# Dhidden products two hidden chunks ahead, `kvbd` transposed on TensorE instead of by DMA, and loads respread around the last MLP chunk, in a fused transformer-block backward kernel

## Chip, cores, metric

One core of one Trainium2 chip. The metric is the device time of one execution in microseconds. Timed comparisons run both kernels alternately on the same chip. Several chips were used, so times are compared only within one set of rounds. Each run also has a mean granted clock of TensorE, 1.000 being full; a loss of 1.7 us out of 860 shows there as 0.998.

## The reference

One pre-norm block on 2048 tokens of width 640: linear attention with 32 heads, then a SwiGLU MLP with 1728 hidden units. The kernel returns the block's output and, for a given `grad_out`, the gradients of `x` and of all five weights, in bf16.

```python
def _fwd_reference(A_x, A_wqkv, A_wo, B_x, B_w1, B_w3, B_w2):
    # A: qkv = x @ wqkv; phi(t) = where(t > 0, t + 1, exp(t)) + 1e-6
    #    kv = sum_s phi(k) v ; o = phi(q) kv / (phi(q) z) ; return o @ wo
    # B: h = silu(x @ w1) * (x @ w3) ; return h @ w2
    h = x + _A_ref(_layernorm(x), A_wqkv, A_wo)
    return h + _B_ref(_layernorm(h), B_w1, B_w3, B_w2)

_out, _vjp = jax.vjp(_f, A_x, A_wqkv, A_wo, B_w1, B_w3, B_w2)
return (_out, *_vjp(grad_out))
```

## The kernel before

The instruction order of every engine is written out by hand. These stages matter here:

1. q, k, v and the key-value sums (0 to 76 us). The sums are kept as `kvbd`, where a mask leaves each head only its own block.
2. The first attention outputs: token tiles 0 to 3, mixed with the last q tiles (76 to 101 us). Each tile goes through a chain over several engines: `nd` on TensorE, `o_t` on VectorE, transpose on TensorE, `oT` on ScalarE, `at` on TensorE, statistics and `hn` on VectorE, transpose `trh` on TensorE.
3. The MLP in four token chunks `c` of 512, each in 14 hidden chunks `fc` of 128 (f chunks), with the gradient through the activation (101 to 360 us). "dhidden product" below means `w2T` times the transposed `grad_out`, five matmuls of 512 columns (`mlp_ghh`).
4. The gradient of `w2`, called `gw` (360 to 420 us). It reads `hb`, the hidden activations loaded transposed. The inputs of stage 5 are loaded meanwhile: `w13a` and `w13b` (the transposed `w1` and `w3`, with a small remainder called the tail), `kvbdT` (the transposed `kvbd`), and `ggb` (the gradients that stage 3 stored in DRAM as `gg_d`).
5. The gradients through the MLP's first product (`ghn`) and through the attention, token tile by token tile (424 to 600 us).
6. The remaining weight gradients and the gradient of `x`.

All plain DMA loads and most DMA transposes (`dmaT`) are issued in order from SyncE's queue.

```python
# stage 1: once, at the start
V.memset(kvbd[:], 0.0)
make_mask()                                  # GpSimd: one memset, ten selects
...
# stage 2: the hand-written order of the first attention outputs
for f, t in ((q_late, 8), (q_late, 9), (f2_ndo, 0), (q_late, 10), (f2_ot, 0), (f2_ndo, 1), (q_late, 11),
             (f2_at0, 0), (f2_ot, 1), (f2_ndo, 2), (q_late, 12), (f2_hn, 0), (f2_at0, 1), (f2_ht, 0),
             ...
             (q_late, 14), (f2_hn, 2), (f2_at0, 3), (f2_ht, 2), (q_late, 15), (f2_hn, 3)):
    f(t)
mlp_ghh(0, 0)
f2_ht(3)
mlp_ghh(0, 1)
...
# stage 3
def mlp_ghh(c, fc):
    acc = mm5(w2T, fc, g2T[c])               # PSUM tag "mm", three buffers
    if fc % 2 == 0:
        ghh[fc // 2] = ew("ghh")
    A.copy(out=ghh[fc // 2][:, fc % 2, :], in_=acc[:])

def mlp(c, fc, between, done):
    if fc not in done:
        mlp_ghh(c, fc)
    gp = mm5(w1, fc, hnT[c])
    ...                                      # sig, s2, gate on ScalarE
    upp = mm5(w3, fc, hnT[c])
    A.copy(out=up[:, i, :], in_=upp[:])      # up: two buffers, stored to DRAM by SyncE
...
if fc == (9 if c == 0 else 3) and c + 1 < SC:
    load_g2T(c + 1)                          # DMA transpose of the next chunk's grad_out
if c == SC - 1 and fc == 0:
    for i in range(SC):                      # grad_out, 640 KB each
        dma(out=g2[:, i * TPC:(i + 1) * TPC, :], in_=goS[:, i * TPC:(i + 1) * TPC, :])
if c == SC - 1 and fc == 4:
    dmaT(out=woT[:], in_=A_wo[:, :])
...
# stage 4, in the loop over fc of the gradient of w2
if fc == 2:
    for m in range(DT):
        kvbd_T(m)                            # five DMA transposes
if fc == 3:
    load_hh(3)                               # DMA transpose
if fc == 5:
    load_w13()                               # two small tail loads, two large DMA transposes
if fc == 8:
    load_gg(0, 0, NG)                        # ggb, what ghn waits for
```

Of the kernel before, what the change touches and what calls it, by code (L numbers as in the profile page):

```python
# [9 lines left out]
P = 128  # L10
BF16 = mybir.dt.bfloat16
F32 = mybir.dt.float32
ALU = mybir.AluOpType
# [6 lines left out]
DH = D // H  # L20
DA = DH + 1
# [42 lines left out]
def kernel(  # L64
# [105 lines left out]

    mask = cp.tile([P, DT, M_MAX], BF16, name="mask")

    def make_mask():
        G.memset(mask[:], 1.0)
        for m, (a, b) in enumerate(M_H):
            v = mask[:, m, 0:M_W[m]].rearrange("p (h e) -> p h e", e=DA)

            G.affine_select(out=v, in_=v, pattern=[[-DH, b - a], [0, DA]], compare_op=ALU.is_ge, fill=0.0,
                            base=m * P - a * DH, channel_multiplier=1)
            G.affine_select(out=v, in_=v, pattern=[[DH, b - a], [0, DA]], compare_op=ALU.is_gt, fill=0.0,  # L180
                            base=a * DH + DH - m * P, channel_multiplier=-1)


    w1 = U2.tile([P, DT, FP], BF16, name="w1", tag="A")
# [4 lines left out]
    g2T = {}  # L189

    def load_g2T(c):
        g2T[c] = U2.tile([P, DT, W], BF16, name="g2T", bufs=2)
        dmaT(out=g2T[c][:], in_=goD[c * W:(c + 1) * W, :])

    def load_pqT(c):
# [88 lines left out]
    p1_norm(0)  # L284
    p1_tr(0)
    ln1.run(x_sb, 1, 2)
    V.memset(kvbd[:], 0.0)
    p1_norm(1)
    ln1.run(x_sb, 2, 4)
    make_mask()  # L290
    trickle += [lambda: dmaT(out=w2T[:, :, 0:F], in_=B_w2[:, :]), lambda: load_g2T(0)]
    for c0, c1 in ((0, 2), (2, 4), (4, 5)):
        trickle += load_w13(c0, c1)
# [3 lines left out]
    for t in range(ST):  # L297
        g, i = divmod(t, TPC)
        if i == 0:
            pkc[g] = p1.tile([P, TPC, D], BF16, name="pkc", bufs=2)  # L300
        k = p1_mm(t, D)
        if t + 2 < ST:
            p1_norm(t + 2)
        phi(k, pkc[g][:, i, :])
        if t + 1 < ST:
            p1_tr(t + 1)
        if i == 0 and g > 0:
            kv_group(g - 1, False)
        v = p1_mm(t, 2 * D)
        A.copy(out=va[g % 2][:, i, 0:C].rearrange("p (j h e) -> p j h e", j=2, e=DA)[:, :, :, 0:DH],  # L310
               in_=v[:, :, 0:HD].rearrange("p j (h e) -> p j h e", e=DH))
        if 4 <= t < 12:
            q_tile(t - 4)
        if t % 2 == 0 and t + 4 < ST:
            ln1.run(x_sb, t + 4, t + 6)
        if i == TPC - 1:
            sl = slice(g * TPC, (g + 1) * TPC)
            dma(out=pk_v[:, sl, :], in_=pkc[g][:])
            dma(out=va_v[:, sl, :], in_=va[g % 2][:])
        elif t >= 2 and trickle:  # L320
            trickle.pop(0)()
# [90 lines left out]
    def mm5(w, fc, rhs):  # L412
        acc = ps.tile([P, W], F32, name="mm", bufs=3)
        for c in range(DT):
            T.matmul(acc[:], lhsT=w[:, c, fc * P:(fc + 1) * P], rhs=rhs[:, c, :], start=(c == 0),  # L415
                     stop=(c == DT - 1))
        return acc

    def ew(name):
        return pa.tile([P, 2, W], BF16, name=name, bufs=2)  # L420
# [1 line left out]
    NAMES = ("sig", "s2", "gate", "up")  # L422
    ghh, pair = {}, {}

    def mlp_ghh(c, fc):
        acc = mm5(w2T, fc, g2T[c])
        if fc % 2 == 0:
            ghh[fc // 2] = ew("ghh")
        A.copy(out=ghh[fc // 2][:, fc % 2, :], in_=acc[:])  # L429

    def mlp(c, fc, between, done):

        k, i = divmod(fc, 2)
        if fc not in done:
            mlp_ghh(c, fc)
        gp = mm5(w1, fc, hnT[c])
        if i == 0:
            pair[k] = [ew(name) for name in NAMES]
        sig, s2, gate, up = pair[k]
        A.activation(sig[:, i, :], gp[:], AF.Sigmoid)  # L440
        A.activation(s2[:, i, :], gp[:], AF.Sigmoid, scale=-1.0)
        A.copy(out=gate[:, i, :], in_=gp[:])
        drain(1)
        between()
        drain(1)
        if fc < FT - 1:
            upp = mm5(w3, fc, hnT[c])
            A.copy(out=up[:, i, :], in_=upp[:])
        else:
            V.memset(up[FL:, i, :], 0.0)  # L450
            A.copy(out=up[:FL, i, :], in_=gp[FL:])
        if i == 1:
            mlp_pair(c, k, *pair.pop(k), ghh.pop(k))

    def store(dst, r0, c, k, src):
        cs = slice(c * W, (c + 1) * W)
# [58 lines left out]
        f2_nd(t)  # L515
        f2_o(t)

    for f, t in ((q_late, 8), (q_late, 9), (f2_ndo, 0), (q_late, 10), (f2_ot, 0), (f2_ndo, 1), (q_late, 11),
                 (f2_at0, 0), (f2_ot, 1), (f2_ndo, 2), (q_late, 12), (f2_hn, 0), (f2_at0, 1), (f2_ht, 0),
                 (f2_ot, 2), (f2_ndo, 3), (q_late, 13), (f2_hn, 1), (f2_at0, 2), (f2_ht, 1), (f2_ot, 3),  # L520
                 (q_late, 14), (f2_hn, 2), (f2_at0, 3), (f2_ht, 2), (q_late, 15), (f2_hn, 3)):
        f(t)
    p1.release()
    pa = pool("pa", "right")
    mlp_ghh(0, 0)
    f2_ht(3)
    mlp_ghh(0, 1)

    w2 = U1.tile([P, FT, D], BF16, name="w2", tag="D")
    V.memset(w2[64:, FT - 1, :], 0.0)  # L530

    def sides(tr):
        side = ({}, {})
        for i in range(TPC):
            k0 = 3 * i - (tr and i == TPC - 1)
            for k, pos, f in ((k0, 0, f2_ndo), (k0 + 1 - tr, 1, f2_ot), (k0 + 2, 1, f2_at), (k0 + 3, 0, f2_hn),
                              (k0 + 4 - tr, tr, f2_ht)):
                side[pos].setdefault(k, []).append((f, i))
        return side

    sides = sides(1)
    for c in range(SC):
        hhT[c] = pa.tile([P, FT, W], BF16, name="hhT", bufs=2)
        o2 = o2_steps(c - 1) if c > 0 else None

        def run_side(pos, fc):
            if c + 1 < SC:
                for f, i in sorted(sides[pos].get(fc, ()), key=lambda x: x[1]):
                    f((c + 1) * TPC + i)

        for fc in range(FT):
            mlp(c, fc, lambda: run_side(0, fc), (0, 1) if c == 0 else ())
            drain(1)
            if o2 and not (c == SC - 1 and fc == 5):
                next(o2, None)
            run_side(1, fc)
            drain(1)
            if c == 0 and fc in (1, 4, 7):
                a, b = {1: (0, 4), 4: (4, 8), 7: (8, 13)}[fc]
                dma(out=w2[:, a:b, :], in_=B_w2[a * P:b * P, :].rearrange("(c p) n -> p c n", p=P))  # L560
                if fc == 7:
                    dma(out=w2[0:FL, FT - 1, :], in_=B_w2[(FT - 1) * P:F, :])
            if fc == (9 if c == 0 else 3) and c + 1 < SC:
                load_g2T(c + 1)
            if c == SC - 1 and fc == 0:
                g2 = U1.tile([P, ST, D], BF16, name="g2", tag="Q")
                for i in range(SC):
                    dma(out=g2[:, i * TPC:(i + 1) * TPC, :], in_=goS[:, i * TPC:(i + 1) * TPC, :])
            if c == SC - 1 and fc == 4:
                woT = U1.tile([P, DT, D], BF16, name="woT", tag="W6")  # L570
                dmaT(out=woT[:], in_=A_wo[:, :])
    drain(1)
# [21 lines left out]
    load_hh(1)  # L594
    load_hh(2)
    wT = [U1.tile([P, FT, D], BF16, name="w13a", tag="D"), U1.tile([P, FT - 1, D], BF16, name="w13b", tag="S0")]
    tail = br.tile([P, DT, P], BF16, name="w13tail")

    def load_w13():
        dma(out=tail[:, :, 0:FL], in_=B_w1[:, F - FL:F].rearrange("(c p) f -> p c f", p=P))  # L600
        dma(out=tail[:, :, FL:P], in_=B_w3[:, 0:P - FL].rearrange("(c p) f -> p c f", p=P))
        dmaT(out=wT[0][:, 0:FT - 1, :], in_=B_w1[:, 0:F - FL])  # L602
        dmaT(out=wT[1][:], in_=B_w3[:, P - FL:F])  # L603

# [5 lines left out]

    kvbdT = br.tile([P, CT, D], BF16, name="kvbdT")

    def kvbd_T(m):
        dmaT(out=kvbdT[:, :, m * P:(m + 1) * P], in_=kvbd[:, m, :])

    ggb = {}

# [26 lines left out]
    for fc in range(FT - 1):  # L644
        b, i = divmod(fc, 4)
        if fc == FT - 2:
            sb = gw2_tail()
        acc = ps.tile([P, 2, 512], F32, name="gw", bufs=4)
        for j in range(2):
            for t in range(ST):  # L650
                T.matmul(acc[:, j, 0:HD], lhsT=hb[b][:, t, i * P:(i + 1) * P], rhs=g2[:, t, j * HD:(j + 1) * HD],  # L651
                         start=(t == 0), stop=(t == ST - 1))
            if fc == FT - 2 and j == 0:
                gw2_tail_out(sb)
        ob = br.tile([P, D], BF16, name="gw2o", bufs=2)
        A.copy(out=ob[:].rearrange("p (j n) -> p j n", j=2), in_=acc[:, :, 0:HD])
        A.dma_start(out=out_6[fc * P:(fc + 1) * P, :], in_=ob[:])
        if fc == 3:
            load_hh(3)
        if fc == 5:  # L660
            load_w13()
        if fc == 8:
            load_gg(0, 0, NG)
        if fc == 11:
            load_gg(1, 0, NG)
        if fc == 2:
            for m in range(DT):
                kvbd_T(m)
        if fc == FT - 3:
            w13_tail()  # L670
    ps.release()
# [457 lines left out]
```

## Time and profile before

| | kernel before |
|---|---|
| median of 3 runs | 864.53 us (863.66 to 865.08) |
| profiled span | 862.8 us |
| TensorE busy | 842.6 us |
| VectorE, ScalarE busy | 416.1, 322.8 us |
| longest waits of TensorE after the start | 3.2 (`ggb`), 2.3 (`up`) us |

How to read it: TensorE's busy time comes within 20.2 us of the span. The lines are shown in the prediction. A timeline line has start and length in us, then engine, line of the kernel, operation and tiles; `SPq` is the issuing on SyncE's queue, and brackets hold the idle time before and what ended it. A line that starts with a window ends with the granted clock, the DMA share and GB/s.

### The profile page before, as it was taken

Reading aid. Unit: us, or ns where it says so; the run is one execution under the profiler, and the core shown is the slowest. Engines: PE = TensorE matmul, PEld = TensorE weight load, DVE = VectorE, ACT = ScalarE, POOL = GpSimd, SP = SyncE. Lnnn points to the kernel's source line nnn. Section 1 sums busy time; section 2 is a strip of 40 time slices with the busy share of each in tenths; the row PEclk is TensorE's granted clock in tenths of the full one; section 3 lists DMA queues with packets and bytes.
Section 4 is the critical chain, followed back from the end, with each engine's and each line's share of the span. In section 5 each row is a group of like instructions: output and inputs, shape, how many; then the busy total and the mean of one; then the engine's idle time right before and its main releaser. Section 6 shows DMA issues by size and latency. Waiting matters only on the chain.

```text
span 862.8 us, 14882 instructions
## 1 busy us (share of the span) xinstructions
PE 842.6 (98%) x5936; PEld 545.9 (63%) x5936; DVE 416.1 (48%) x940; ACT 322.8 (37%) x608; POOL 25.0 (3%) x42
## 2 busy tenths in 40 slices
PE   6999999999999899999899999999999999999998
PEld 4777544555555455777577777777877777655554
DVE  7786599877778465300045666664413333300000
ACT  4556866655555566011121112122522333311111
POOL 3100000000000000000000000000000000000000
PEclk9999999999999999999999999999999999999999
DMA  9979579365374652999969999959866988667671
GB/s 293 245 240 272 153 207 241 115 178 144 96 184 130 216 143 101 219 224 220 276 132 181 228 195 200 192 119 242 203 123 119 195 196 156 169 150 174 142 182 36
DMA packets 343573, 156.03 MB, mean 181 GB/s; under 512 B 246224, under 2 KB 342224, under 8 KB 343504
## 3 DMA queue, kind: packets, MB, share of 16 engines
q1 hardware_dynamic: 314688, 142.12, 68.7%
q10 hardware_dynamic: 28816, 12.97, 8.1%
q8 instruction: 46, 0.75, 0.4%
q14 instruction: 23, 0.19, 0.1%
HBM read 45.20 MB, written 50.02 MB: 110 GB/s over the span
## 4 chain that ended last, share of the span: by engine, by line
PE 77%; DMA 5%; SPq 3%; DVE 2%; ACT 1%; issue 0%; ACTq 0%; DVEq 0%
PE job L960 21%; PE mm L415 19%; PE ghn L708 10%; PE gxn L1050 8%; PE o L500 7%; PE gw L651 3%; PE gwo L815 3%; DMA ghT<-g_h 2%; PE h L765 2%; PE at L372 2%; SPq L602 1%; DMA ggb<-gg_d 1%; SPq L603 1%; DMA gg_d<-up 1%; DMA kT<-pk_d 1%; PE dkv L1009 1%
## 5 line engine op out<-in xcount | busy, mean ns | idle before, releaser
L960 PE MATMUL job<-gb,hnN 128*128 128x432 bf16 x640 | 117.0, 346 | 0.0
L708 PEld LDWEIGHTS <-ggb 128*128 128x128 bf16 x864 | 83.7, 98 | 35.3 <-DMA ggb<-gg_d 3.5
L960 PEld LDWEIGHTS <-hnN 128*128 128x128 bf16 x640 | 62.6, 98 | 54.1
L415 PE MATMUL mm<-pqT,w 128*128 128x512 bf16 x405 | 96.2, 379 | 0.0
L415 PEld LDWEIGHTS <-w 128*128 128x128 bf16 x540 | 52.4, 98 | 63.5 <-issue 2.8
L964 ACT CAST obs<-job 128x432 bf16<-128x432 f32 (+1 forms) x70 | 33.3, 476 | 123.8 <-PE job L960 123.8
L708 PE MATMUL ghn<-w13a,ggb 128*128 128x320 bf16 x448 | 67.2, 304 | 3.2 <-DMA ggb<-gg_d 3.2
L415 PE MATMUL mm<-g2T,w2T 128*128 128x512 bf16 x280 | 69.6, 379 | 0.0
L500 PE MATMUL o<-w,hhT 128*128 128x320 bf16 x448 | 67.5, 299 | 0.0
L1050 PE MATMUL gxn<-wqT,gT 128*128 128x320 bf16 x480 | 67.3, 299 | 0.0
L708 PE MATMUL ghn<-w13b,ggb 128*128 128x320 bf16 x416 | 63.5, 299 | 0.0
L225 PE MATMUL big<-wqkv,pqT 128*128 128x320 bf16 x400 | 59.0, 306 | 0.8 <-ACT pqT L221 0.8
L500 PEld LDWEIGHTS <-hhT 128*128 128x128 bf16 x448 | 43.8, 98 | 23.6
L225 PEld LDWEIGHTS <-pqT 128*128 128x128 bf16 x480 | 46.7, 99 | 18.7 <-ACT pqT L221 1.0
L1050 PEld LDWEIGHTS <-gT 128*128 128x128 bf16 x480 | 47.0, 98 | 18.2
L960 PEld LDWEIGHTS <-g 128*128 128x128 bf16 x480 | 46.6, 98 | 17.5
L651 PE MATMUL gw<-g,hb 128*128 128x320 bf16 x416 | 57.0, 299 | 0.0
L429 ACT CAST ghh<-mm 128x512 bf16<-128x512 f32 x56 | 32.8, 586 | 64.3 <-PE mm L415 35.6
L731 ACT ACTIVATE y<-wb,s,ln_rs 128x640 bf16<-128x640 f32 x32 | 29.4, 920 | 66.5 <-DVE wb L727 66.5
L651 PEld LDWEIGHTS <-hb 128*128 128x128 bf16 x416 | 40.6, 98 | 15.7
L719 ACT ACTIVATE gs<-ghn 128x640 bf16<-128x640 f32 x16 | 11.3, 704 | 90.6 <-PE ghn L708 81.8
L415 PEld LDWEIGHTS <-w2T 128*128 128x128 bf16 x280 | 27.4, 98 | 25.6
(135 smaller groups left out, 1066.4 us busy)
## 6 DMA issues: line engine op xcount, KB each, us to landing
hh_d<-hhT SPq DMA_DIRECT2D x24, 256.0 KB, 2.4
gg_d<-gate SPq DMA_DIRECT2D x24, 256.0 KB, 2.5
gg_d<-up SPq DMA_DIRECT2D x24, 256.0 KB, 2.2
ggb<-gg_d SPq DMA_DIRECT2D x6, 896.0 KB, 8.7
ggb<-gg_d SPq DMA_DIRECT2D x6, 832.0 KB, 7.5
out_dram<-obs ACTq DMA_DIRECT2D x40, 108.0 KB, 2.3
ggb<-gg_d SPq DMA_DIRECT2D x2, 1728.0 KB, 13.4
va_d<-va SPq DMA_DIRECT2D x4, 768.0 KB, 6.0
```

Of the source, the lines that this page charges most:

```text
L225: T.matmul(acc, lhsT=pqT[:, c, t * P:(t + 1) * P], rhs=wqkv[:, c, n0:n0 + HD], start=(c == 0), stop=(c == DT - 1))
L372: T.matmul(at[:, 0:HD], lhsT=oT[t][:, c, :], rhs=wo[:, c, j * HD:(j + 1) * HD], start=(c == 0 and not on_pe), stop=(c == DT - 1))
L415: T.matmul(acc[:], lhsT=w[:, c, fc * P:(fc + 1) * P], rhs=rhs[:, c, :], start=(c == 0), stop=(c == DT - 1))
L429: A.copy(out=ghh[fc // 2][:, fc % 2, :], in_=acc[:])
L500: T.matmul(o2["ps"][:, 0:HD], lhsT=hhT[c][:, fc, i * P:(i + 1) * P], rhs=w2[:, fc, j * HD:(j + 1) * HD], start=(fc == 0), stop=(fc == FT - 1))
L651: T.matmul(acc[:, j, 0:HD], lhsT=hb[b][:, t, i * P:(i + 1) * P], rhs=g2[:, t, j * HD:(j + 1) * HD], start=(t == 0), stop=(t == ST - 1))
L708: T.matmul(acc[:, j, 0:HD], lhsT=ggb[t // 2][:, k, lo:lo + P], rhs=rhs[:, j * HD:(j + 1) * HD], start=(k == 0), stop=(k == NG - 1))
L731: A.activation(out=y[:], in_=wb[:], func=AF.Identity, bias=s[:, 3:4], scale=st.rs[:, t:t + 1])
L815: T.matmul(acc[m][:, j, 0:HD], lhsT=o_sb[:, t, m * P:(m + 1) * P], rhs=g_h[:, t, j * HD:(j + 1) * HD], start=(t == 0), stop=(t == ST - 1))
L960: T.matmul(acc[:, 0:n], lhsT=lhs[:, t, m * P:(m + 1) * P], rhs=rhs(t), start=(t == 0), stop=(t == ST - 1))
L964: A.copy(out=ob, in_=acc[:, 0:n])
L1050: T.matmul(acc[:, j, 0:HD], lhsT=gT[t][:, k, :], rhs=wqT[:, k, j * HD:(j + 1) * HD], start=(k == 0), stop=(k == 14))
```

## The change

The intent is to give TensorE something to do while it waits, and to keep transfers from standing in front of others that are needed first.

```diff
-    def make_mask():              # all at the start
+    def make_mask(m):             # one fifth in each of the iterations 2 to 6
-    V.memset(kvbd[:], 0.0)
+            G.memset(kvbd[:, t - 2, :], 0.0)
...
+    AHEAD = 2
-        if fc not in done:
-            mlp_ghh(c, fc)
+        n = c * FT + fc
+        if n >= FILL - AHEAD:     # FILL = 4
+            mlp_ghh(n + AHEAD)    # its result tile ghh gets three buffers instead of two
...
-    ... (q_late, 10), (f2_ot, 0), (f2_ndo, 1), (q_late, 11), ... (q_late, 12), (f2_hn, 0), (f2_at0, 1), (f2_ht, 0), ...
+    ... (q_late, 10), (mlp_ghh, 0), (f2_ot, 0), ... (f2_hn, 0), (q_late, 12), (f2_at0, 1), (mlp_ghh, 1), (f2_ht, 0), ...
+    ... (f2_hn, 3), (q_late, 15), (mlp_ghh, 2), (f2_ht, 3), (mlp_ghh, 3)
...
-                for i in range(SC):          # at fc == 0
-                    dma(out=g2[:, i * TPC:(i + 1) * TPC, :], ...)
-            if c == SC - 1 and fc == 4:      # woT
+            if c == SC - 1 and fc in (1, 2, 5, 6):
+                i = (1, 2, 5, 6).index(fc)
+                dma(out=g2[:, i * TPC:(i + 1) * TPC, :], ...)
+            if c == SC - 1 and fc == 8:
+                dma(out=tail[:, :, 0:FL], ...)      # before: in load_w13
+                dma(out=tail[:, :, FL:P], ...)
+            if c == SC - 1 and fc == 9:      # woT
...
-        dmaT(out=kvbdT[:, :, m * P:(m + 1) * P], in_=kvbd[:, m, :])
+        for i, dc in enumerate(dcs):
+            T.transpose(tr[:, i, :], kvbd[:, dc, cc * P:(cc + 1) * P], ident[:])
+        V.tensor_copy(out=kvbdT[:, cc, ...], in_=tr[:])
-        if fc == 2:
-            for m in range(DT):
-                kvbd_T(m)
+        if fc < CT:
+            kvbd_T(*BLOCKS[fc])
```

Of the schedule of the later chunks the diff rewrites the helper `sides` too, but for the arguments it is called with it returns the same schedule.

More of the change, by code (lines that the diff above doesn't have):

```diff
@@ L171 @@
     mask = cp.tile([P, DT, M_MAX], BF16, name="mask")
-    def make_mask():
-        G.memset(mask[:], 1.0)
-        for m, (a, b) in enumerate(M_H):
-            v = mask[:, m, 0:M_W[m]].rearrange("p (h e) -> p h e", e=DA)
-            G.affine_select(out=v, in_=v, pattern=[[-DH, b - a], [0, DA]], compare_op=ALU.is_ge, fill=0.0,
-                            base=m * P - a * DH, channel_multiplier=1)
-            G.affine_select(out=v, in_=v, pattern=[[DH, b - a], [0, DA]], compare_op=ALU.is_gt, fill=0.0,
-                            base=a * DH + DH - m * P, channel_multiplier=-1)
+    def make_mask(m):
+        a, b = M_H[m]
+        v = mask[:, m, 0:M_W[m]]
+        G.memset(v, 1.0)
+        v = v.rearrange("p (h e) -> p h e", e=DA)
+        G.affine_select(out=v, in_=v, pattern=[[-DH, b - a], [0, DA]], compare_op=ALU.is_ge, fill=0.0,
+                        base=m * P - a * DH, channel_multiplier=1)
+        G.affine_select(out=v, in_=v, pattern=[[DH, b - a], [0, DA]], compare_op=ALU.is_gt, fill=0.0,
+                        base=a * DH + DH - m * P, channel_multiplier=-1)
     w1 = U2.tile([P, DT, FP], BF16, name="w1", tag="A")
@@ L191, in load_g2T @@
     def load_g2T(c):
-        g2T[c] = U2.tile([P, DT, W], BF16, name="g2T", bufs=2)
+        g2T[c] = U2.tile([P, DT, W], BF16, name="g2T", tag="g2T", bufs=2)
         dmaT(out=g2T[c][:], in_=goD[c * W:(c + 1) * W, :])
@@ L286 @@
     ln1.run(x_sb, 1, 2)
-    V.memset(kvbd[:], 0.0)
     p1_norm(1)
     ln1.run(x_sb, 2, 4)
-    make_mask()
     trickle += [lambda: dmaT(out=w2T[:, :, 0:F], in_=B_w2[:, :]), lambda: load_g2T(0)]
@@ L315 @@
             ln1.run(x_sb, t + 4, t + 6)
+        if 2 <= t < 2 + DT:
+            make_mask(t - 2)
+            G.memset(kvbd[:, t - 2, :], 0.0)
         if i == TPC - 1:
@@ L423, with mlp_ghh, mlp @@
     ghh, pair = {}, {}
-    def mlp_ghh(c, fc):
-        acc = mm5(w2T, fc, g2T[c])
-        if fc % 2 == 0:
-            ghh[fc // 2] = ew("ghh")
-        A.copy(out=ghh[fc // 2][:, fc % 2, :], in_=acc[:])
-    def mlp(c, fc, between, done):
+    def mlp_ghh(n):
+        if n < SC * FT:
+            c, fc = divmod(n, FT)
+            acc = mm5(w2T, fc, g2T[c])
+            if n % 2 == 0:
+                ghh[n // 2] = pf.tile([P, 2, W], BF16, name="ghh", bufs=3)
+            A.copy(out=ghh[n // 2][:, n % 2, :], in_=acc[:])
+    AHEAD = 2
+    def mlp(c, fc, between):
         k, i = divmod(fc, 2)
-        if fc not in done:
-            mlp_ghh(c, fc)
+        n = c * FT + fc
+        if n >= FILL - AHEAD:
+            mlp_ghh(n + AHEAD)
         gp = mm5(w1, fc, hnT[c])
@@ L452, in mlp @@
         if i == 1:
-            mlp_pair(c, k, *pair.pop(k), ghh.pop(k))
+            mlp_pair(c, k, *pair.pop(k), ghh.pop(n // 2))
     def store(dst, r0, c, k, src):
@@ L516, in f2_ndo @@
         f2_o(t)
-    for f, t in ((q_late, 8), (q_late, 9), (f2_ndo, 0), (q_late, 10), (f2_ot, 0), (f2_ndo, 1), (q_late, 11),
-                 (f2_at0, 0), (f2_ot, 1), (f2_ndo, 2), (q_late, 12), (f2_hn, 0), (f2_at0, 1), (f2_ht, 0),
-                 (f2_ot, 2), (f2_ndo, 3), (q_late, 13), (f2_hn, 1), (f2_at0, 2), (f2_ht, 1), (f2_ot, 3),
-                 (q_late, 14), (f2_hn, 2), (f2_at0, 3), (f2_ht, 2), (q_late, 15), (f2_hn, 3)):
+    FILL = 4
+    for f, t in ((q_late, 8), (q_late, 9), (f2_ndo, 0), (q_late, 10), (mlp_ghh, 0), (f2_ot, 0), (f2_ndo, 1), (q_late, 11),
+                 (f2_at0, 0), (f2_ot, 1), (f2_ndo, 2), (f2_hn, 0), (q_late, 12), (f2_at0, 1), (mlp_ghh, 1), (f2_ht, 0),
+                 (f2_ot, 2), (f2_ndo, 3), (f2_hn, 1), (q_late, 13), (f2_at0, 2), (f2_ht, 1), (f2_ot, 3), (f2_hn, 2),
+                 (q_late, 14), (f2_at0, 3), (f2_ht, 2), (f2_hn, 3), (q_late, 15), (mlp_ghh, 2), (f2_ht, 3), (mlp_ghh, 3)):
         f(t)
@@ L524, with sides @@
     pa = pool("pa", "right")
-    mlp_ghh(0, 0)
-    f2_ht(3)
-    mlp_ghh(0, 1)
     w2 = U1.tile([P, FT, D], BF16, name="w2", tag="D")
     V.memset(w2[64:, FT - 1, :], 0.0)
-    def sides(tr):
+    def sides(late):
         side = ({}, {})
         for i in range(TPC):
-            k0 = 3 * i - (tr and i == TPC - 1)
-            for k, pos, f in ((k0, 0, f2_ndo), (k0 + 1 - tr, 1, f2_ot), (k0 + 2, 1, f2_at), (k0 + 3, 0, f2_hn),
-                              (k0 + 4 - tr, tr, f2_ht)):
+            k0 = 3 * i - (i == TPC - 1)
+            for k, pos, f in ((k0, 0, f2_ndo), (k0, 1, f2_ot), (k0 + 2, 1, f2_at), (k0 + 3, 0, f2_hn),
+                              (k0 + 3, 1, f2_ht)):
+                if late and f is f2_at and i != late - 1:
+                    k, pos = k + 1, 0
                 side[pos].setdefault(k, []).append((f, i))
         return side
-    sides = sides(1)
+    sides = [sides(0), sides(0), sides(0)]
     for c in range(SC):
@@ L547, in run_side @@
             if c + 1 < SC:
-                for f, i in sorted(sides[pos].get(fc, ()), key=lambda x: x[1]):
+                for f, i in sorted(sides[c][pos].get(fc, ()), key=lambda x: x[1]):
                     f((c + 1) * TPC + i)
         for fc in range(FT):
-            mlp(c, fc, lambda: run_side(0, fc), (0, 1) if c == 0 else ())
+            mlp(c, fc, lambda: run_side(0, fc))
             drain(1)
@@ L566 @@
                 g2 = U1.tile([P, ST, D], BF16, name="g2", tag="Q")
-                for i in range(SC):
-                    dma(out=g2[:, i * TPC:(i + 1) * TPC, :], in_=goS[:, i * TPC:(i + 1) * TPC, :])
-            if c == SC - 1 and fc == 4:
+                tail = U2.tile([P, DT, P], BF16, name="w13tail", tag="g2T", bufs=2)
+            if c == SC - 1 and fc in (1, 2, 5, 6):
+                i = (1, 2, 5, 6).index(fc)
+                dma(out=g2[:, i * TPC:(i + 1) * TPC, :], in_=goS[:, i * TPC:(i + 1) * TPC, :])
+            if c == SC - 1 and fc == 8:
+                dma(out=tail[:, :, 0:FL], in_=B_w1[:, F - FL:F].rearrange("(c p) f -> p c f", p=P))
+                dma(out=tail[:, :, FL:P], in_=B_w3[:, 0:P - FL].rearrange("(c p) f -> p c f", p=P))
+            if c == SC - 1 and fc == 9:
                 woT = U1.tile([P, DT, D], BF16, name="woT", tag="W6")
@@ L596 @@
     wT = [U1.tile([P, FT, D], BF16, name="w13a", tag="D"), U1.tile([P, FT - 1, D], BF16, name="w13b", tag="S0")]
-    tail = br.tile([P, DT, P], BF16, name="w13tail")
     def load_w13():
-        dma(out=tail[:, :, 0:FL], in_=B_w1[:, F - FL:F].rearrange("(c p) f -> p c f", p=P))
-        dma(out=tail[:, :, FL:P], in_=B_w3[:, 0:P - FL].rearrange("(c p) f -> p c f", p=P))
         dmaT(out=wT[0][:, 0:FT - 1, :], in_=B_w1[:, 0:F - FL])
@@ L611, with kvbd_T @@
     kvbdT = br.tile([P, CT, D], BF16, name="kvbdT")
-    def kvbd_T(m):
-        dmaT(out=kvbdT[:, :, m * P:(m + 1) * P], in_=kvbd[:, m, :])
+    def kvbd_T(cc, dcs):
+        tr = ps.tile([P, len(dcs), P], BF16, name="trk", tag="gw", bufs=4)
+        for i, dc in enumerate(dcs):
+            T.transpose(tr[:, i, :], kvbd[:, dc, cc * P:(cc + 1) * P], ident[:])
+        V.tensor_copy(out=kvbdT[:, cc, dcs[0] * P:(dcs[-1] + 1) * P].rearrange("p (i q) -> p i q", q=P), in_=tr[:])
     ggb = {}
```

## The prediction

> **What bounds the kernel now.** I read the page's busy times first, then the waits of TensorE, then the timeline around each of those waits, then the granted clock around the longest of them.
>
> ```profile
> PE 842.6 (98%) x5936; PEld 545.9 (63%) x5936; DVE 416.1 (48%) x940; ACT 322.8 (37%) x608; POOL 25.0 (3%) x42
> ...
> PE   6999999999999899999899999999999999999998
> ```
>
> TensorE is busy for 842.6 of 862.8 us, so it is the bound, and at most 862.8 - 842.6 = 20.2 us of idle time can be taken out without taking matmuls out. The change removes no matmul. So the whole question is which of these 20.2 us go, and what is added. Stretches of 25 us tell where they lie: 6.7 in 0 to 25 (5.7 of it before the first transpose can run), 2.8 in 75 to 100, 0.3 in 125 to 150, 1.8 and 0.5 in 275 to 325, 3.4 in 400 to 425, 1.3 in three stretches of 450 to 575, and 3.2 after the last matmul.
>
> ```profile
> PE tr L219 <- DVE xn L145: 5.9, 2, 5.7
> PE ghn L708 <- DMA ggb<-gg_d: 3.2, 1, 3.2
> PE mm L415 <- ACT up L448: 2.3, 1, 2.3
> PE trh L409 <- DVE hn L145: 1.9, 4, 0.8
> PE tr L360 <- DVE o_t L348: 0.9, 1, 0.9
> ```
>
> These are TensorE's waits (total us, times, longest). Lines 2 to 5, 8.3 us, are each the target of one part of the change. Where does the 2.3 of the third line come from?
>
> ```profile
> 287.55 2.54 SPq L568 DMA_DIRECT2D g<-in_grad_out_dram  x4
> ...
> 290.18 1.45 SPq L461 DMA_DIRECT2D gg_d<-up  x1
> ...
> 299.87 0.59 ACT L448 CAST up<-mm 128x512 bf16<-128x512 f32 x1 [4.21 <-DMA gg_d<-up]
> ...
> 300.51 1.24 PE L415 MATMUL mm<-hnT,w 128*128 128x512 bf16 x5 [2.32 <-ACT up L448]
> ```
>
> Four grad_out loads of 640 KB are issued at once; the store of `up` queued behind them lands about 9.7 us after its issue instead of the usual 2.2, ScalarE can't overwrite `up`, PSUM fills, TensorE stops. And the 3.2:
>
> ```profile
> 358.82 19.29 SPq L582 DMA_TRANSPOSE hb<-hh_d  x2
> ...
> 378.21 7.74 SPq L614 DMA_TRANSPOSE kvbdT<-kvbd  x5
> ...
> 386.05 4.10 SPq L582 DMA_TRANSPOSE hb<-hh_d  x1
> ...
> 391.40 11.08 SPq L602 DMA_TRANSPOSE w13a<-in_B_w_dram  x1
> ...
> 402.58 10.28 SPq L603 DMA_TRANSPOSE w13b<-in_B_w_dram  x1
> ...
> 412.91 6.25 SPq L621 DMA_DIRECT2D ggb<-gg_d  x2
> ...
> 423.56 4.84 PE L708 MATMUL ghn<-w13a,ggb 128*128 128x320 bf16 x22 [3.18 <-DMA ggb<-gg_d]
> ```
>
> SyncE's queue has no hole from 358.8 to 413: the load that the next stage waits for is issued at the moment the transposes ahead of it are through. That is also what the chain that ended last says there. The gap costs more than its 3.2 us, as the clock of the same place shows (column before DMA share is the granted clock):
>
> ```profile
> 424.00:426.00 2.00, 2.00 (x13) 1.31 (x11) 0.00 (x0) 0.69 (x1) 0.00 (x0) 0.70 1.21 290
> 426.00:428.00 2.00, 2.00 (x10) 1.08 (x8) 0.00 (x0) 0.00 (x0) 0.00 (x0) 0.50 1.19 295
> 428.00:430.00 2.00, 2.00 (x15) 1.42 (x14) 0.00 (x0) 0.00 (x0) 0.00 (x0) 0.95 0.68 240
> ```
>
> TensorE counts as busy here, but at 0.70, 0.50 and 0.95 of full speed: 2 x (0.30 + 0.50 + 0.05) = 1.7 us lost inside "busy".
>
> **What the Trainium skill says.** "TensorE: Matmul & The Clock Gate", Part 1 (What's actually happening): the array's clock falls to half after about one idle window of 3.4 us and returns after about as long a busy one. The trace agrees at 424 to 430; after the gap of 2.3 us at 298 the clock stayed at 1.00, so only the longer gap pays. "DMA: Bandwidth & Descriptors", Anatomy of one DMA: semaphore waits happen on the issuing sequencer, not on the DMA engines. The trace agrees as far as it goes: what stands ahead on SyncE's queue delays everything behind it. The same page, Latency and other measured facts, gives 261 GB/s for a DMA transpose with a non-contiguous middle dimension; here 640 x 1664 x 2 bytes took 11.08 us of issue, 192 GB/s, so the trace's own durations are used. "SBUF — State Buffer", SBUF: two separate sides, says that GpSimd and some VectorE instructions exclude each other on a shared port; the trace has the normalisation `xn` at 0.88 us beside the GpSimd memset of the mask against 0.44 elsewhere. So GpSimd work moved later can slow VectorE there.
>
> **The change part by part.**
>
> 1. Start. VectorE loses the 1.66 us memset of `kvbd`; GpSimd's mask work leaves the first 17 us for the iterations 2 to 6, with about 0.7 us more per iteration for `kvbd` (estimate from 840 elements in 0.80 us). TensorE's first 5.7 us wait for the first load, statistics and normalisation, none of which changes. The memset lies in the shadow of the first ten matmuls (7.18 to 10.03), and the second `xn` is done before they end. Only the 0.2 us wait at 17.1 can go. In 25 to 75 TensorE has no idle time and VectorE 19.1 and 17.5 of 25, which absorbs some port conflicts. Gain 0.2.
>
> 2. First attention outputs, 78 to 100. The gaps are 0.93 (transposes of `o_t`), 0.50, 0.20, 0.41 and 0.75 (transposes of `hn`): 2.8 us. A dhidden product is five matmuls of 216 ns, 1.08 us. One now stands before the first, one before the second, one before the last gap; for the others `hn` is normalised before the two VectorE operations of the q tile (0.33 + 0.49 us) instead of after. Each filler is longer than its gap. Two of the four products stood there already, after the gaps. Against it: ScalarE is busy 3.2 of 4 us here and gets two more evictions of 0.5 us. I count 2.5 of 2.8. The look-ahead itself is neutral: five matmuls less in each of the last two f chunks of the MLP. The rewritten schedule of the later chunks comes out the same for its arguments.
>
> 3. grad_out loads. One 640 KB load at each of the f chunks 1, 2, 5, 6 is about 2 us of transfer (estimate from the DMA's 363 GB/s at 296 to 298) in 4.3 us of MLP, so no store stands behind 7 us of it. Gain 2.3. `woT` and the tail move to f chunks 8 and 9; `woT` blocks the queue for 3.65 us, which at f chunk 4 stopped nothing on TensorE.
>
> 4. The transposes after the MLP. SyncE's queue loses 7.74 us (`kvbdT`) and 1.2 us (the tail's two issues, 390.2 to 391.4). The third `hb` transpose needs TensorE to be done with four f chunks, 360.3 + 4 x 4.35 = 377.7, so it can follow at 378.2 without a hole. Then `ggb` is issued 7.74 + 1.2 = 8.9 us earlier, at about 404, and lands at about 404 + 10.6 = 414.6 in the old time base, against 420.4 when TensorE is free for it. The wait has 5.8 us of slack: gain 3.2, and the clock stays up: gain 1.7.
>
> 5. Added: 12 transposes on TensorE (as many as the later group L999 has), about 60 ns each in a stream (five take 0.44 us with some 0.2 of latency): 12 x 0.06 = 0.7, say 0.8 us, all on the path as TensorE is the bound. Six VectorE copies lie where VectorE does nothing.
>
> Sum: 0.2 + 2.5 + 2.3 + 3.2 + 1.7 - 0.8 = 9.1 us. 864.5 - 9.1 = 855.4.
>
> **Rivals.** (a) PSUM takes over as the wait: the transposes take tiles from the same four as the weight gradient, so an accumulator must be evicted about one f chunk (4.35 us) after its end. ScalarE is late there now: one ended at 377.7 was evicted at 381.4, because output stores wait. For it: that lateness; against: the large transposes end 9 us sooner. It could cost 1 to 3 us: 857 to 858. (b) The first `hb` transpose becomes the wait. It is issued at 348.46, takes 11.7 us to land in the median, and TensorE starts on it at 360.2 with no idle time, so it is nearly a tie. The last two f chunks become 1.08 us shorter each, and VectorE, which had 2.4 us to spare before the last pair, has almost none. If the store of `hh` slips, TensorE waits 0.5 to 1.5 us: 856 to 857. (c) ScalarE binds in the attention part and gives back half of step 2: 856.7. (d) The clock loss was not tied to the gap and comes back elsewhere: 857. (e) Better than the sum: the earlier end of the DMA backlog also removes the 0.7 us wait for `ghT` at 454, and there is no loss of step 2: 854.
>
> **Range and chances.** The upside is capped: with steps 1 to 4 complete and no cost of step 5 it is 10.2 us, 854.3, plus (e). The downside is one or two of (a) to (d). So 855.4, with 852.8 to 859 for 8 in 10. Two per cent is 17.3 us, which nearly the whole idle time would have to yield; slower by 2% would need a new stall of 26 us, for which I see no transfer large enough. Faster 0.02, same 0.96, slower 0.02.
>
> **What would show it.** In the changed profile: no wait of `ghn` for `ggb`, and a clock of 1.00 through the start of that stage (step 4); no wait of `mm` for `up` (step 3); the waits of `trh` and `tr` for `hn` and `o_t` gone or under 0.4 us together (step 2); a new group of 12 transposes `trk` in the weight-gradient stage and TensorE busy lower by about 1 us, the regained clock less the transposes (step 5); the first wait still 5.7 us (step 1). A new wait of `trk` or `gw` for ScalarE would show (a), of `gw` for `hb` would show (b), and of `mm` for an eviction before 105 us (c). The prediction is wrong if `ggb` is still issued near 412, or if the total leaves the range.

## The result, and the profile after

| rounds | before, median | after, median | ratio (95%) |
|---|---|---|---|
| first comparison | 864.81 us (4 runs) | 855.87 us (4 runs) | 0.9894 (0.9864 to 0.9924) |
| repeated, another chip | 861.03 us (11 runs) | 854.12 us (6 runs) | 0.9924 (0.9905 to 0.9942) |

A ratio is the mean time of one kernel's runs over that of the other's of the same rounds, so not quite the ratio of the medians. Executions over 1.5% slower than the fastest of the same kernel are left out of the means. Both comparisons show a clear gain that is under 2%: 8.9 us in the first and 6.9 us in the second, by the medians.

The page of the changed kernel begins:

```profile
span 851.9 us, 14886 instructions
...
PE 838.2 (98%) x5920; PEld 545.6 (64%) x5948; DVE 416.4 (49%) x945; ACT 322.2 (38%) x608; POOL 29.1 (3%) x51
```

This profiled run was the fastest of its four (854.0 us). A few matmul records are missing from it (5920 matmuls against 5948 weight loads), so TensorE's busy sum is somewhat too low, and the prediction's sign "TensorE busy lower by about 1 us" can't be read from it. The waits are the safer reading (total us, times, longest):

```profile
PE tr L220 <- DVE xn L145: 5.7, 1, 5.7
PE big L226 <- ACT pqT L222: 0.8, 1, 0.8
PE mm L417 <- DMA g2T<-in_grad_out_dram: 0.7, 1, 0.7
PE ghn L720 <- DMA ggb<-gg_d: 0.4, 1, 0.4
PE big L226 <- DVE pkc L242: 0.4, 1, 0.4
PE at L374 <- DVE o_t L350: 0.4, 1, 0.4
PE h L777 <- DMA ghT<-g_h: 0.3, 1, 0.3
```

The waits of `trh`, `tr` (for `o_t`) and `mm` (for `up`) are gone. The wait of `ghn` at the start of its stage is gone as well: the 0.4 us that is left falls at 490 us. Two waits are new. One is `mm` for `g2T`, the transposed `grad_out` of the next chunk. The other is that of `big` for `pkc`, 0.43 us at 17.2 us (0.41 in the second profile); it takes the place of the 0.20 us wait for `xn` at 17.1 us that was to go. SyncE's queue ahead of `ggb`, and TensorE's first work on it:

```profile
353.06 23.59 SPq L596 DMA_TRANSPOSE hb<-hh_d  x3
...
376.70 10.70 SPq L612 DMA_TRANSPOSE w13a<-in_B_w_dram  x1
...
387.49 10.61 SPq L613 DMA_TRANSPOSE w13b<-in_B_w_dram  x1
...
398.21 5.51 SPq L634 DMA_DIRECT2D ggb<-gg_d  x2
...
415.25 3.97 PE L720 MATMUL ghn<-w13a,ggb 128*128 128x320 bf16 x28
```

`ggb` is issued 17.0 us before `ghn` starts, against 10.65 us in the kernel before, and `ghn` starts without a wait. Its first 28 matmuls take 3.97 us; in the kernel before the same 28 took 5.65 us. The clock of that place (third column from the right) is full:

```profile
414.00:416.00 2.00, 2.00 (x17) 1.44 (x15) 0.00 (x0) 0.32 (x1) 0.00 (x0) 1.00 0.63 205
416.00:418.00 2.00, 2.00 (x17) 1.43 (x16) 0.00 (x0) 0.38 (x1) 0.00 (x0) 1.00 0.49 127
```

Where the time went can be told stage by stage from the start of the first instruction of each stage on TensorE. The table has two profiles of each kernel (the second ones are from the experiments), in us:

| stretch, by its first instructions | before | before, again | after | after, again |
|---|---|---|---|---|
| start to first `nd` | 76.47 | 76.61 | 76.38 | 76.28 |
| to the first `w1` product (first attention outputs) | 24.36 | 24.35 | 22.95 | 22.95 |
| to the first `w2` product (MLP chunk 0) | 53.33 | 53.26 | 54.10 | 54.47 |
| to the first `w1` product of chunk 3 | 130.09 | 130.09 | 130.09 | 130.09 |
| to the first `gw` (MLP chunk 3) | 76.07 | 76.03 | 71.43 | 71.81 |
| to the first `ghn` (gradient of `w2`) | 63.24 | 61.85 | 60.30 | 60.30 |
| to the first `gwo` (tile loop) | 148.88 | 147.44 | 146.47 | 145.72 |
| to TensorE's end | 287.11 | 287.12 | 287.11 | 287.12 |

Two dhidden products, 2.16 us, moved from chunk 3 into the attention part. So, in the first profiles, the attention part gained 1.41 + 2.16 = 3.57 us, and chunk 3 gained 4.64 - 2.16 = 2.48 us. Chunk 0 lost 0.77 us.

### The profile page after: what moved, and what is told of

The parts are those of the page before. It is cut to its first block, busy times and chain, and to the rows that moved or that the text cites. A ratio compares the mean times of both kernels' runs of the same rounds, so it can differ in the third digit from the quotient of the medians.

```text
span 851.9 us, 14886 instructions
## 1 busy us (share of the span) xinstructions
PE 838.2 (98%) x5920; PEld 545.6 (64%) x5948; DVE 416.4 (49%) x945; ACT 322.2 (38%) x608; POOL 29.1 (3%) x51
## 4 chain that ended last, share of the span: by engine, by line
PE 85%; DMA 3%; DVE 2%; ACT 1%; issue 0%; SPq 0%; DVEq 0%; ACTq 0%
PE job L972 21%; PE mm L417 18%; PE ghn L720 11%; PE gxn L1062 8%; PE o L508 7%; PE gw L664 7%; PE gwo L827 3%; PE h L777 2%; PE at L374 2%; DMA ghT<-g_h 1%; DMA ggb<-gg_d 1%; PE mm L226 1%; PE dkv L1021 1%; DMA g2T<-in_grad_out_dram 1%; PE dkv L808 1%; PE h L808 1%
## 5 line engine op out<-in xcount | busy, mean ns | idle before, releaser
L448 ACT ACTIVATE sig<-mm 128x512 bf16<-128x512 f32 x56 | 33.5, 598 | 28.9 <-PE mm L417 27.0
```

Source lines behind the costliest of these rows:

```text
L448: A.activation(sig[:, i, :], gp[:], AF.Sigmoid)
```

## The experiments

**Theory.** The gain is the sum of independent waits that end: the short ones in the attention part, the one behind the `grad_out` loads, and the one for `ggb`, which is set by the order of SyncE's queue; after a wait the clock may be lowered, and that loss goes with the wait. **Rivals.** The gain in the `gw` stage comes from fewer DMA bytes and not from the order; the clock has nothing to do with the gaps; the look-ahead gives its gain back elsewhere.

### only_fill: the look-ahead and the new attention order alone

```diff
 kernel before, with only
+        if n >= FILL - AHEAD: mlp_ghh(n + AHEAD)
+    the order with (mlp_ghh, 0) to (mlp_ghh, 3) and the earlier (f2_hn, t)
```

> The kernel before with the look-ahead and the new order of the first attention outputs alone. My theory: TensorE's waits for o_t and hn in the first attention outputs (2.8 us in the kernel before) go, but the product that needs the second grad_out transpose is now asked for three f chunks after its load is issued and waits about 0.7 us for it, as in the changed kernel; net gain 2.0 to 2.5 us, ratio 0.997 to 0.998. Rival: ScalarE's two extra evictions give back half of it; gain 1.0 to 1.4 us, and waits of mm for ScalarE before 105 us.

Measured: 859.56 us against 862.83 (ratio 0.9964, 0.9940 to 0.9987). The attention part took 22.95 us, exactly as in the changed kernel, and its waits for `o_t` and `hn` are gone. The waits of TensorE hold what was given back:

```profile
PE ghn L713 <- DMA ggb<-gg_d: 2.8, 1, 2.8
PE mm L415 <- DMA g2T<-in_grad_out_dram: 1.5, 1, 1.5
```

The stretch of chunk 0 took 54.94 us instead of 53.33. The loss is the wait for `g2T`: the look-ahead asks for the next chunk's `grad_out` two f chunks earlier, and the load had not been moved. The rival with ScalarE falls: no wait of `mm` for ScalarE lies before 105 us. The gain by the medians, 3.3 us, is a little above the expected 2.0 to 2.5, but the interval of the ratio holds the expected range too, so the excess is not clear of noise. This run doesn't separate the look-ahead from the earlier `hn` in the new order.

### only_g2: the grad_out loads alone

```diff
-            if c == SC - 1 and fc == 0: (four loads)
+            if c == SC - 1 and fc in (1, 2, 5, 6): (one load each)
```

> The kernel before with the four grad_out loads spread over the f chunks 1, 2, 5, 6 alone. Theory: the store of up lands in about 2 to 4 us instead of 9.7, the 2.3 us wait of mm for ScalarE at about 298 us is gone, gain 2.3 us, nothing else moves. Rival: the stop only moves to a later store, and a wait of 0.5 us or more of mm for up stays somewhere between 290 and 345 us.

Measured: 861.53 against 862.83 us (ratio 0.9987, 0.9966 to 1.0007), so the time alone doesn't settle it. The profile does: no wait of `mm` for ScalarE is left, and chunk 3 took 73.60 us instead of 76.07, which is 2.47 us less. The rival falls. By the medians the gain is 1.3 us; the interval holds the expected 2.3 us as well. That the wait is often shorter is seen in other profiles: where nothing that comes before 298 us was touched, the wait for `up` was 2.32, 2.28, 2.2, 1.7, 1.7 and 0.6 us. It is not the same in every execution, and its mean here, 1.8, is below the 2.3 of the first profile. Four of the six runs had a mean clock of 0.998 or less; the gap before `ghn` was still there (2.60 us in the profile).

### only_kvbdT: kvbd on TensorE alone

```diff
-        if fc == 2: five DMA transposes
+        if fc < CT: kvbd_T(*BLOCKS[fc])     # T.transpose and a VectorE copy
```

> The kernel before with kvbd transposed on TensorE instead of by five DMA transposes, alone. Theory: SyncE's queue reaches the ggb loads 7.7 us earlier, near 405; the 3.2 us wait of ghn and the 1.7 us of lowered clock after it are gone, 0.7 us of transposes are added; gain 4.2 us, ratio near 0.995. Rival A (clock not tied to the gap): only 2.5 us. Rival B (PSUM tiles shared with the weight gradient make TensorE wait for evictions): a wait of gw or trk for ScalarE or VectorE, gain under 3 us.

Measured: 859.11 against 862.83 us; five of six runs between 858.85 and 861.39, one at 865.8 (ratio 0.9978, 0.9947 to 1.0009, so again the profile has to settle it). No wait of `ghn` for `ggb` is left, and the stage took 60.29 us. Rival B falls: neither `gw` nor `trk` waits for ScalarE or VectorE. On rival A the runs are mixed: four of six had a mean clock of 1.000, two had 0.996 and 0.998 although this gap was gone from the profile; the one at 298 us was still there (2.21 us). That was taken up below.

### only_tail: the tail loads alone

```diff
-        dma(out=tail[:, :, 0:FL], ...); dma(out=tail[:, :, FL:P], ...)   # in load_w13
+            if c == SC - 1 and fc == 8: the same two loads
```

> The kernel before with the two tail loads moved into the last MLP chunk, alone. Theory: the queue is 1.2 us shorter, so the wait of ghn shrinks from 3.2 to about 2.0 us. Whether the clock drops after such a gap is the point: in the kernel before it stayed at 1.00 after a gap of 2.3 us and dropped after 3.2. If it stays up here, gain 2.9 us and the clock 1.00 in the 6 us after the gap; if it drops again, gain 1.2 us and about 0.7, 0.5, 0.95.

Measured: 862.69 against 862.83 us (ratio 0.9998, 0.9973 to 1.0022), so no gain is shown. In the profile the wait at the start of `ghn` was 1.66 us with a clock of 1.00 after it, but a second wait of 1.55 us for `ggb` came at 457 us:

```profile
PE ghn L710 <- DMA ggb<-gg_d: 3.2, 2, 1.7
```

Three of the six runs had a mean clock of 0.998. They had the gap at 298 us too and left no profile, so which gap lowered their clock is not known. Alone, this part is worth nothing that five rounds can see.

### gg_first: the same wait, taken away by order alone

```diff
         if fc == 5:
+            load_gg(0, 0, NG)
             load_w13()
-        if fc == 8:
-            load_gg(0, 0, NG)
```

> The kernel before with one line moved: the first ggb load stands ahead of the two large weight transposes in SyncE's queue instead of behind them. Nothing is removed. Theory (the order of the queue alone makes the wait): ggb lands before 415, no wait of ghn for ggb, and the later weight transposes still land before they are needed (w13a about 412, w13b about 421 to 424); gain 3.2 us plus the clock where it drops. Rival (the DMA engines are full, whatever goes first): ghn or a later matmul of it waits for w13b instead, 1 us or more, and the gain is under 2 us.

Measured: 860.37 against 863.55 us (ratio 0.9956, 0.9936 to 0.9977), a gain of 3.2 us by the medians.

```profile
389.19 0.59 SPq L621 DMA_DIRECT2D ggb<-gg_d  x1
...
395.09 12.42 SPq L602 DMA_TRANSPOSE w13a<-in_B_w_dram  x1
...
419.87 3.97 PE L707 MATMUL ghn<-w13a,ggb 128*128 128x320 bf16 x28
```

`ghn` waits for nothing at its start, and the `gw` stage took 59.63 us. No transfer was removed here; the bytes are the same and SyncE's queue is as full as before. So the order of the queue makes the wait, and the rival falls. Another wait took some of the gain in this profile:

```profile
PE h L764 <- DMA ghT<-g_h: 1.5, 1, 1.5
```

The 59.63 us, the same in both profiles of this kernel, are also the measure of the stage without any wait. Against them the changed kernel's 60.30 us show what the 12 transposes cost on TensorE: 0.67 us, or 56 ns each.

### after_d5 and after_d8: transposes put back into the queue

```diff
 changed kernel, with
+        if fc == 6:
+            for m in range(5):     # or 8
+                dmaT(out=kvbdT[:, :, m % DT * P:(m % DT + 1) * P], in_=kvbd[:, m % DT, :])
```

> The changed kernel with five DMA transposes of kvbd put back into the queue ahead of the ggb loads (they write the same values that TensorE's transposes wrote, so the result stays right); TensorE's own transposes stay. Theory: ggb is issued 7.7 us later, near 406, and lands near 416.5; ghn is ready at 415.3, so a wait of 0 to 2 us comes back, without a loss of clock: 0 to 2 us slower than the changed kernel. Rival (removed DMA bytes, not the queue's order, made the gain): the weight-gradient stage itself gets longer by more than the wait.

Measured: 856.43 against 863.55 us (ratio 0.9900, 0.9870 to 0.9931). The wait of `ghn` at its start is 0.52 us, within the 0 to 2 us expected, and the `gw` stage took 60.98 us: 60.30 and the wait, within 0.2. So in this stage five DMA transposes cost nothing beside their place in the queue. This kernel also showed the tie that the prediction names as rival (b): `gw` waited 1.1 us for the first `hb`.

> As the run with five, with eight DMA transposes. Theory: ggb is issued 12.4 us later, near 410.6, and lands near 421; a wait of 5 to 6 us of ghn comes back, and as it is longer than any seen so far the clock drops to 0.5 after it, costing 1.7 us or more; 6.5 to 9 us slower than the changed kernel, so about as slow as the kernel before less 2. If the clock stays at 1.00 after such a wait, the clock has nothing to do with the gap.

Measured: 861.31 against the same 863.55 us (ratio 0.9972, 0.9934 to 1.0010), 4.9 us slower by the median than the run with five. The waits, and the clock around the gap:

```profile
PE ghn L723 <- DMA ggb<-gg_d: 5.5, 2, 4.8
```

```profile
422.00:424.00 2.00, 2.00 (x8) 1.17 (x9) 0.00 (x0) 0.00 (x0) 0.00 (x0) 0.53 1.21 291
424.00:426.00 2.00, 2.00 (x11) 1.22 (x10) 0.00 (x0) 0.00 (x0) 0.00 (x0) 0.62 1.16 295
426.00:428.00 2.00, 2.00 (x17) 1.46 (x15) 0.00 (x0) 0.00 (x0) 0.00 (x0) 1.00 0.80 257
```

The gap of 4.76 us begins at 417.23; from 422 on the clock is about half for some 3.5 us, a loss of 2 x (0.47 + 0.38) = 1.7 us. All four runs had a mean clock of 0.998. The gap and the lowered clock are both back, by transfers alone. The gap was foretold at 5 to 6 us. The total looks smaller than the foretold 6.5 to 9 us: no run of the changed kernel shared this chip, but by the ratios (0.9972 against 0.9894 and 0.9924) the cost is 4 to 7 us. With four runs and an interval of 0.9934 to 1.0010 no more can be said.

### before_a: the kernel before, once more

```diff
 (no edit)
```

> The kernel before, once more, for its profile. The waits of its single profile vary: the wait for up was 2.3 there and 2.2, 0.6 and 0.5 us in three kernels that don't touch it before that point; the wait for ggb was 3.2 there and 2.6 and 2.8 in two that don't touch it, with a clock of 1.00 after both. If the loss of clock is a matter of the gap's length with an edge near 3 us, a gap below 3 here leaves the clock at 1.00, one above lowers it.

Measured: one run, 861.75 us.

```profile
422.19 2.23 PE L708 MATMUL ghn<-w13a,ggb 128*128 128x320 bf16 x9 [2.07 <-DMA ggb<-gg_d]
```

```profile
422.00:424.00 2.00, 1.80 (x9) 1.11 (x10) 0.00 (x0) 0.69 (x1) 0.00 (x0) 0.65 1.21 290
424.00:426.00 2.00, 2.00 (x9) 1.16 (x8) 0.00 (x0) 0.00 (x0) 0.00 (x0) 0.50 1.21 290
```

A gap of 2.07 us was followed by a lowered clock, while gaps of 2.60 (the grad_out run) and 2.78 us (the look-ahead run) were not, nor was the 2.3 us gap at 298 us in the two profiles of the kernel before. So my idea of an edge near 3 us is wrong: the length of the gap alone doesn't decide. Where the clock fell, the loss was the same: 1.7 us in the first profile, 2 x (0.35 + 0.50) = 1.7 here, and 1.7 with eight transposes.

### after_again: the changed kernel with more rounds

```diff
 (the changed kernel, no edit)
```

> The changed kernel again, with more rounds, beside the next runs on the same chip. Ratio to the kernel before 0.987 to 0.992, and a mean clock of at least 0.999 in all six runs, against about half of the runs of the kernel before at 0.998 or lower (12 of 22 so far). The wait of mm for the second grad_out transpose near 143 us is there again, 0.7 to 1.6 us, as in the four profiles that have the look-ahead.

Measured: 854.12 against 861.03 us (ratio 0.9924, just outside the expected 0.987 to 0.992). All six runs had a mean clock of 1.000, as had the four of the first comparison. Of the kernel before, 16 of all 33 runs that were timed beside the experiments had 0.998 or less. Within one chip those runs were slower than its other runs by 2.7, 2.4 and 1.5 us on the three chips. That difference may hold more than the clock, since a run with longer gaps would be slower too. The wait for `g2T` was there again with 1.1 us.

### kvbdT_g2: the two long gaps away, the short ones kept

```diff
 kernel before, with the edits of only_kvbdT and only_g2
```

> The kernel before with two parts of the change, kvbd transposed on TensorE and the grad_out loads spread; no look-ahead, and the tail stays. Both long gaps (298 and 420 us) are gone, the five short ones of the first attention outputs stay. Two theories for the lowered clock, which also came in 3 of 6 runs with ggb first and 2 of 6 with kvbd on TensorE alone: if the gap at 298 us causes it there, all six runs here have a clock of 0.999 or more, and the ratio is 0.991 to 0.994. If short gaps (0.5 to 1.5 us) before or after cause it too, one to three runs have 0.998 or less, and the ratio is 0.993 to 0.996.

Measured: 856.79 against 861.03 us (ratio 0.9950, 0.9936 to 0.9963). All six runs had a mean clock of 1.000. The short waits are still there:

```profile
PE trh L409 <- DVE hn L145: 1.9, 4, 0.8
PE tr L360 <- DVE o_t L348: 0.9, 1, 0.9
```

So the five short gaps of the attention part do not lower the clock in these runs. The first theory is right about the clock and too hopeful about the time: 4.2 us by the medians, where its ratio meant 5 to 8. On this chip only 4 of 11 runs of the kernel before had the lowered clock to lose, which explains a part at most; the rest stays open. Against this run the changed kernel is 2.7 us faster on the same chip. That is the part of the look-ahead with its new order, together with the tail and the start.

### gg_first_b: one more look for the place

```diff
 (as gg_first)
```

> The kernel with the first ggb load ahead of the weight transposes, once more, for its profile: in half of its runs the clock was lowered although no wait for ggb was left. If this profile has a mean clock under 0.999, the stretch with the lowered clock follows the 1.7 to 2.3 us wait for up at 298 us (theory), or a wait of h for ghT at about 450 us (rival). If it is at 1.000, nothing is learnt about the place.

Measured: one run, 862.54 us, mean clock 1.000, so nothing was learnt about the place. Its profile has a wait of 1.85 us for `ghT` and one of 1.93 us for `ggb` at 552 us: the tile loop took 151.1 us, which is 5 us more than in the best profile here, with no edit in that loop. Between the two profiles of this one kernel the loop alone makes 3.8 us (147.29 and 151.10), and the spans differ by 3.3. Where the clock fell in 3 of the 6 runs of that kernel stays open. The gap at 298 us is the suspect, because it is the long gap that these runs still had.

### g2T_8: the new wait attacked

```diff
 changed kernel, with
-            if fc == (9 if c == 0 else 3) and c + 1 < SC:
+            if fc == (8 if c == 0 else 3) and c + 1 < SC:
                 load_g2T(c + 1)
```

> The changed kernel with the second grad_out transpose issued after f chunk 8 of the first MLP chunk instead of after 9. Theory: the wait near 143 us is a load asked for three f chunks ahead that takes 5 us behind other DMAs; one f chunk more (about 3.5 us) removes it; the stretch from the first product of the MLP to the first of the second chunk goes from 54.1 to 54.9 us back to 53.3 to 53.6; 0.7 to 1.5 us faster than the changed kernel. Rival: issued earlier it stands in front of the transposes of o_t, and at waits for oT instead; no gain.

Measured: 854.84 us, against 854.12 of the changed kernel in the same rounds (ratio to before 0.9933, 0.9911 to 0.9955), so no gain. The wait for `g2T` is gone and another stands in its place:

```profile
PE mm L417 <- ACT up L456: 0.8, 1, 0.8
```

```profile
134.02 3.80 SPq L194 DMA_TRANSPOSE g2T<-in_grad_out_dram  x1
137.92 0.53 SPq L467 DMA_DIRECT2D gg_d<-up  x1
...
142.01 0.59 ACT L456 CAST up<-mm 128x512 bf16<-128x512 f32 x1 [3.13 <-DMA gg_d<-up]
```

Issued earlier, the 3.8 us transpose stands in front of the store of `up`; ScalarE waits for that store before it can overwrite `up`, and PSUM fills. It is the mechanism of the 298 us gap on a smaller scale. Chunk 0 took 54.22 us, no better than the 54.10 and 54.47 with the load at its old place. One of the six runs had a mean clock of 0.998, with neither of the two long gaps in its program; that run has no profile here, so what lowered its clock stays open. Neither the theory nor the named rival was right: the cost moved to a store and not to `oT`. No version was found that is faster than the changed kernel.

## Why the prediction was right

The predicted 855.4 us lies 0.5 us from the first measured median, and the range held both medians of the changed kernel. The second median is from a chip on which the kernel before was 3.8 us faster (861.03 against 864.81), so there it is the gain that compares: 6.9 us, where 9.1 were foretold. That the first gain, 8.9 us, came so near is partly luck, because the prediction took the sizes of its terms from one profile, and they vary. By the medians the four parts that ran alone gave 3.3, 1.3, 3.7 and 0.1 us, 8.4 in all (the start and the move of `woT` were not run alone). That agrees with a plain sum of the parts, though each is uncertain by 2 to 3 us. By the prediction's own steps:

1. **Start, 0.2 us.** The first `nd` came at 76.38 and 76.28 us against 76.47 and 76.61: about 0.2, too small to tell from the start's own variation. The first wait is 5.7 us as foretold, but the 0.2 us wait that was to go was replaced by one of 0.4 us for `pkc`. No run has this part alone.
2. **Attention part, 2.5 us.** The mechanism was right and two sizes were off that happen to cancel. The part gained 3.57 us, more than the 2.8 us of idle time. An estimate of why: a gap also costs the filling of the pipeline after it (five transposes take 0.44 us to their end, while in a stream the next work begins 0.28 us after their start; five gaps of 0.16 us more make up the difference). But the statement that the look-ahead itself is neutral failed. It asks for `g2T` earlier; chunk 0 lost 0.8 and 1.2 us in the two profiles of the changed kernel. Net 2.8 and 2.4 us. Rival (c) did not come: no wait of `mm` for ScalarE lies before 105 us.
3. **grad_out loads, 2.3 us.** Right where the wait is present (2.47 us in the run with this part alone). The term was taken from one profile; the wait itself is between 0.6 and 2.3 us from run to run.
4. **The ggb wait, 3.2 + 1.7 us.** The queue argument was right to the microsecond: `ggb` was issued at 398.2, which is 403.6 in the old time base (the stage began 5.4 us earlier), where about 404 was foretold; `ghn` doesn't wait for it, and the run with the order changed shows that order is enough. (The section that the prediction cites for queues is about DMAs issued from GpSimd; for SyncE's queue the evidence is that run.) The size is that of one profile: the wait of the kernel before was 3.18 and 2.07 us, and the lowered clock came in about half of its runs. As a mean the clock term is nearer to half of 1.7. (It lies inside "busy", so the prediction's opening cap of 20.2 us leaves it out.) The sentence "so only the longer gap pays" failed: 2.07 us lowered the clock, and 2.60 and 2.78 did not. What the runs do show is that the long gaps and the lowered clock go together: it came in 16 of 33 runs with both gaps, in 4 of 6 with only the one before `ghn` (only_g2), in 2 of 6 and 3 of 6 with only the one at 298 us (only_kvbdT, gg_first), and in 1 of 26 with neither (the changed kernel 0 of 10, kvbdT_g2 0 of 6, after_d5 0 of 4, g2T_8 1 of 6). So rival (d), that the loss comes back elsewhere, was not seen in the changed kernel.
5. **Transposes on TensorE, 0.8 us added.** Measured 0.67 us.

In the profiled pair the tile loop gave 2.41 us, which the steps had only in part: 1.68 of it is the clock term of step 4 (5.65 less 3.97 us), and the rest goes with shorter waits, as in the prediction's rival (e): `ghT` 0.3 instead of 1.0 us. Rival (a), evictions from PSUM, did not come: ScalarE's copies of `gw` no longer stand behind the stores and mostly wait for TensorE itself,

```profile
ACT gw2o L669 <- PE gw L664: 53.8, 10, 20.4
```

which they did for 29.7 us in 4 instances before. Rival (b) came in small: `gw` waited 0.2 us for `hb` in the second profile of the changed kernel. The chances were right: the time is within 2%.

## What to carry to other kernels

On an engine that is 98% busy, add up the waits that remain and look for what stands ahead of the awaited transfer in its queue: moving one load ahead of the two large transposes gave 3.2 us here without removing any work. When work is moved ahead, move the loads that feed it too, and check what those loads then push back. A wait seen in one profile is a sample: two of the terms here (the wait for `up` and the lowered clock) vary by a factor of two or more between runs, so take a second profile before sizing a gain from it.

## What the Trainium skill lacked or had wrong

- "TensorE: Matmul & The Clock Gate", Why this matters for your kernels, advises "No PE-idle gaps >~3µs between matmul bursts". Here a gap of 2.07 us was followed by a clock of 0.65 and 0.50, while gaps of 2.60 and 2.78 us were followed by 1.00. A gap under 3 us is no guarantee: in the kernel before, whose profiles have two gaps of 2.1 to 3.2 us, 16 of 33 runs had a lowered mean clock, and in the four kernels with neither gap 1 of 26 runs had it. The page's Part 1 ties the fall to an idle window of about 3.4 us, longer than these gaps; no run here shows the window itself.
- The same page, Part 4: PE-mode transpose, gives about 275 ns for a transpose in a kernel's context. A record of the added transposes here is 219 ns, and the 12 transposes placed between matmul streams lengthened their stage by 56 ns each.
- "DMA: Bandwidth & Descriptors", Latency and other measured facts, gives 261 GB/s for a DMA transpose with a non-contiguous middle dimension, from one kernel. The large weight transpose here took 11.08 us of issue for 2.13 MB, 192 GB/s, beside other transfers (225 GB/s in all in that stretch), so this is another case and no proof that the figure is wrong.
- None of the pages that I read says how much a kernel's DMA waits vary from run to run: the tile loop of one and the same kernel took 147.29 and 151.10 us in its two profiles.
